# A chunked state-space scan feeding a two-layer MLP: the exponents of the first ten chunks from rows of cumulated logs

## The chip, the cores and the metric

One core of one Trainium2 chip. The metric is the device time of one execution in microseconds (us). Three runs of the kernel before stand beside the profiled one. Engines go by the profile's names: PE (TensorE; PEld is its weight load), DVE (VectorE), ACT (ScalarE), POOL (GpSimd), SP (the queue that issues nearly all DMAs).

## The reference

Four batches, eight heads, 768 positions, head size 32, state size 16. The scan gives rows of 256 values for 3072 tokens, which an MLP of 2048 hidden values takes in.

```python
log_a = np.log(np.clip(a, 1e-06, 1.0))
for c in range(nc):                        # chunks along the sequence
    cum = np.cumsum(la, axis=-1)           # la: the chunk's logs
    L = np.exp(cum[:, :, :, None] - cum[:, :, None, :]) * causal
    M = np.einsum('bhin,bhjn->bhij', Cc, Bc) * L
    y = M @ xc + (Cc @ state) * np.exp(cum)
    state = exp(sum(la)) * state + (Bc * exp(cum[-1] - cum)).T @ xc
h = x @ w_in                               # x: the scan's rows, 3072 x 256
out = (h - np.tanh(h)) @ w_out             # 256 -> 2048 -> 256
```

## The kernel before

**The scan.** It uses 28 chunks of its own: seven along the sequence for each of the four batches (six of 112 tokens, one of 96), chunk number `ck` counting batches fastest. A chunk's tile has 128 columns of keys: 16 for the carried state, which enters as 16 further tokens, and 112 for its own. For each of the eight heads a 128 x 112 matrix `lt` = exp(cumulated log of the query - that of the key), cut to the causal half, is multiplied by C B^T, and PE multiplies it by the x rows into `y` (L637). The chunks lie in groups of two, which share a load of B and C (`bc`, L265), of x (L277) and of B in rows (`braw`, L286).

Three ways of making `lt` stand side by side:

- *Chunks 0 to 3* (`first_tile`, L435 to L492). POOL lays out each head's logs as a masked 128 x 128 matrix `lm` (L443), four heads at a time; PE writes a mask of -32768 (`eye` times `never`, L448) and adds `lm` times `upto`, a triangle of ones (L451). That gives the differences of the sums, masked, in a PSUM bank (`cp`). ACT takes the exponential (L467), four heads in one instruction; PE makes C B^T in the bank group `att` (L461), and DVE multiplies (L471), again four heads at a time.
- *Chunks 4 to 9* (`chunk_a`, L494). The sums of all chunks are made once as rows (`pr`, L1032), copied, cut by DVE into three bf16 parts (L1042 to L1048), sent to memory (L1051) and fetched back by eight DMAs into `lt_c` and `rt_c` (L1056, L1058), tiles that ACT and DVE have filled with 1 and with 0 or -1 (L991, L995). Four bf16 matmuls of 9 rows each (L507), two heads to a matmul, give the exponents in one half of each of four banks of `att`, and four of 32 rows (L512) C B^T in the other half. ACT takes the exponential of all eight heads (L516), DVE multiplies (L520), POOL zeroes what is not causal (`cut`, L532).
- *Chunks 10 and later* (`chunk_l`, L535) load the rows of sums broadcast from memory, and ACT adds the key's sum as a bias (L550).

**The MLP.** Tiles of tokens, four of 256 and four of 512 columns. `mm1` (L756, L763) multiplies by the first weights into a bank `ph`; ACT takes tanh (L794), DVE subtracts (L798); `mm2` (L834, L844) multiplies by the second weights into `o`. The weights arrive as 64-bit numbers, two halves of each load (`raw`, L296); `conv` (L314) puts them together on ACT (L325) and DVE (L330 to L352). Most products go in three passes of a rounded part and a rest (`wh`, `wl`, `xh`, `xl`). The first tile, with the first two pairs of weight blocks, runs in plain float32 (L756, L834); its x is `xf` (L601). The first four tiles are swept over the weights together, as these come in.

**What sets the order.** Nothing is issued where it is written. Each step is recorded with its engine, an assumed cost and what it reads and writes (`Order.__call__`, L89); `search` (L198) schedules the records 16 times with random disturbance from a seed, keeps the shortest schedule, and issues the steps in that order. `urge` moves a step forward. Each engine then runs its list in order, and waits where data or a buffer is missing. Buffers come in rings: `ph` two banks, `po0` and `po1` one each, `att` one group of four banks, `lt` four, `raw` two, `bc` and `x` three.

## Time and profile before

| | us |
|---|---|
| median of three runs | 324.19 (323.92 to 324.30) |
| the profiled execution's own time | 324.25 |
| its span, first to last instruction | 322.6 |
| outside the span | 1.65 |
| busy in the span: PE, PEld | 313.7, 255.3 |
| busy in the span: DVE, ACT, POOL | 215.3, 210.3, 60.6 |

Busy time counts instructions at work, overlaps once. The timeline gives start, duration, engine, line, what is written and read, and in brackets how long the engine had idled before and what ended that. Where a row has a count, its duration is that of the whole stretch. A float32 matmul is two instructions in the profile (two passes), and one in the program's order; a bf16 or fp32r one is one in both.

### The profile page before, as it was taken

The numbers are of one execution on the slowest core, as the hardware profiler recorded it, in microseconds if no ns is written. First come the engines' busy times: TensorE is split into PE (matmuls) and PEld (weight loads), VectorE is DVE, ScalarE is ACT, GpSimd is POOL, SyncE is SP. The second block draws the span as 40 slices with busy tenths as digits, with TensorE's granted clock in tenths as the row PEclk, the third lists the DMA queues.
The fourth block names the chain that finished last, engine by engine and source line by source line (L and its number), as shares of the span: only waits on it lengthen the run. The fifth ranks groups of instructions, "written<-read, shape, count | busy, mean of one in ns | idle before, by whom it ended". The sixth has DMA issues, their size and how long they took to land.

```text
span 322.6 us, 5757 instructions
## 1 busy us (share of the span) xinstructions
PE 313.7 (97%) x2160; PEld 255.3 (79%) x2160; DVE 215.3 (67%) x314; ACT 210.3 (65%) x471; POOL 60.6 (19%) x94
## 2 busy tenths in 40 slices
...
GB/s 205 195 238 325 173 162 307 183 94 346 89 65 66 30 98 272 48 241 5 205 0 207 16 0 209 1 2 226 168 61 0 2 0 0 68 1 0 2 0 65
DMA packets 15451, 35.27 MB, mean 109 GB/s; under 512 B 2464, under 2 KB 4416, under 8 KB 15424
## 3 DMA queue, kind: packets, MB, share of 16 engines
...
q8 instruction: 17, 0.28, 0.4%
q14 instruction: 10, 0.08, 0.1%
...
## 4 chain that ended last, share of the span: by engine, by line
PE 91%; DVE 5%; ACT 2%; issue 1%
PE ph L763 39%; PE o L844 38%; PE o L834 3%; PE y L704 3%; PE att L678 3%; PE y L637 1%; PE warm L1003 1%; DVE lt L471 1%; ACT lt L550 1%; DVE lt L520 1%; DVE wv L345 1%; PE att L461 1%; PE cp L451 1%; ACT lt L516 1%; DVE wm L338 1%
## 5 line engine op out<-in xcount | busy, mean ns | idle before, releaser
L798 DVE TENSOR_TENSOR g<-ph,g 128x512 f32<-128x512 f32 x96 | 65.7, 688 | 52.1 <-ACT g L794 52.0
L794 ACT ACTIVATE g<-ph 128x512 f32<-128x512 f32 x96 | 57.3, 598 | 48.7 <-PE ph L763 47.8
L808 DVE TENSOR_TENSOR gl<-g,gh 128x512 fp32r<-128x512 f32 x88 | 62.7, 715 | 31.0 <-ACT gh L802 29.5
L763 PE MATMUL ph<-xh,wh 128*128 128x512 f32 (+1 forms) x200 | 76.0, 382 | 0.0
L763 PE MATMUL ph<-xh,wl 128*128 128x512 f32 (+1 forms) x200 | 74.8, 377 | 0.0
L802 ACT CAST gh<-g 128x512 fp32r<-128x512 f32 x88 | 54.4, 620 | 28.3 <-DVE g L798 26.4
L844 PE MATMUL o<-gh,wh 128*128 128x512 f32 x176 | 69.2, 393 | 0.0
L844 PE MATMUL o<-gl,wh 128*128 128x512 f32 x176 | 68.5, 389 | 0.0
L844 PE MATMUL o<-gh,wl 128*128 128x512 f32 x176 | 68.5, 389 | 0.0
L763 PE MATMUL ph<-xl,wh 128*128 128x512 f32 (+1 forms) x200 | 59.0, 376 | 0.0
L532 POOL TENSOR_SCALAR_AFFINE_SELECT lt<-lt 128x896 f32<-128x896 f32 (+1 forms) x24 | 23.3, 969 | 128.4 <-ACT lt L550 118.3
L763 PEld LDWEIGHTS ph<-xh,wh 128*128 128x128 f32 x200 | 37.6, 188 | 7.6 <-issue 0.6
L763 PEld LDWEIGHTS ph<-xh,wl 128*128 128x128 f32 x200 | 37.6, 188 | 6.8
L763 PEld LDWEIGHTS ph<-xl,wh 128*128 128x128 f32 x200 | 36.7, 188 | 7.0
L550 ACT ACTIVATE lt<-lt,ncum 128x112 f32<-128x112 f32 (+1 forms) x144 | 41.7, 375 | 0.0
L844 PEld LDWEIGHTS o<-gh,wh 128*128 128x128 f32 x176 | 33.0, 188 | 7.8 <-issue 0.8
L844 PEld LDWEIGHTS o<-gl,wh 128*128 128x128 f32 x176 | 33.0, 188 | 6.9
L844 PEld LDWEIGHTS o<-gh,wl 128*128 128x128 f32 x176 | 33.1, 188 | 6.7
L684 DVE TENSOR_TENSOR lt<-att,lt 128x896 f32<-128x896 f32 (+1 forms) x18 | 18.9, 1052 | 0.0
L888 POOL DMA_DIRECT2D pt<-part x12 | 11.1, 1023 | 41.1 <-ACT part L885 38.1
L834 PE MATMUL o<-g,wf 128*128 128x256 f32 x64 | 15.4, 384 | 1.4 <-ACT x L578 0.9
L605 ACT CAST xh<-y 128x224 fp32r<-128x224 f32 (+4 forms) x18 | 7.3, 413 | 13.1 <-DVE s L711 10.6
...
## 6 DMA issues: line engine op xcount, KB each, us to landing
...
```

Of the source, the lines that this page charges most:

```text
L532: nc.gpsimd.affine_select(out=k["l"][:, :, 0:q], in_=k["l"][:, :, 0:q], pattern=[[0, H], [1, q]], compare_op=ALU.is_ge, fill=0.0, base=N, ...
L550: nc.scalar.activation(k["l"][:, h, 0:q], k["l"][:, h, 0:q], AF.Exp, bias=ncum[:, h, ck : ck + 1])
L678: nc.tensor.matmul(out=a_[:, i], lhsT=bb[r], rhs=cc[r, :, 0 : qlen(ck)], start=True, stop=True)
L684: nc.vector.tensor_tensor(out=l, in0=chs[j]["a"], in1=l, op=ALU.mult)
L763: nc.tensor.matmul(out=ph[:, i * w : i * w + w], lhsT=w_[:, u, 0, k, j * P : (j + 1) * P], rhs=(xh, xl)[p][:, k, ts], start=p == 0 and k = ...
L794: nc.scalar.activation(g[:, 0:used], gs[t, f][0][:, 0:used], AF.Tanh)
L798: nc.vector.tensor_tensor(out=g, in0=ph, in1=g, op=ALU.subtract)
L802: nc.scalar.copy(gh[:, 0:used], gs[t, f][1][:, 0:used])
L808: nc.vector.tensor_tensor(out=gl[:, 0:used], in0=g[:, 0:used], in1=gh[:, 0:used].bitcast(F32), op=ALU.subtract)
L834: nc.tensor.matmul(out=po[t, seg][e], lhsT=wf[:, u, 256 * j + e * P : 256 * j + (e + 1) * P], rhs=gs[t, f][1][:, i * w : i * w + w], start ...
L844: nc.tensor.matmul(out=po[t, seg][e], lhsT=w_[:, u, 1, j, e * P : (e + 1) * P], rhs=g[:, i * w : i * w + w], start=f == seg[0] and k == 0 ...
L888: op("POOL", 1.0, lambda e=e: nc.gpsimd.dma_start(out=pts[m][:, e], in_=obs[t, e], accum_op=ALU.add), r=[name, n_pt[2 * m], n_pt[2 * m + 1 ...
```

## The change

All ten of the first chunks now go one way; `first_tile`, `lm`, `eye`, `never`, the bf16 parts, their memory copy `cum3` and the ten DMAs that wrote and fetched it are gone.

- `twins`: ACT takes the logs of the first ten chunks a second time into `twin`, each value four times (320 columns).
- `rows_of(g)`, for chunks 0 to 3, 4 to 7 and 8 to 9: four small float32 matmuls per chunk, 32 columns of `twin` times `upto`, put the cumulated logs of each pair of heads at the partitions where the exponents' matmuls read them. For g = 0, ACT writes `lt_c` and DVE `rt_c` (two instructions) straight from that bank, in float32. For g = 1 and 2, ACT first copies a rounded part (`high`), DVE adds the rest for alternate rows (`fn_y`), and ACT and DVE make `lt_c` and `rt_c` in fp32r from the result. Columns of signs and ones (`sel`) choose per partition what becomes a sum and what 1, 0 or -1; DVE makes them with nine small instructions (`sels`).
- `chunk_a` now holds for chunks 0 to 9. `att` is one group of banks for all ten, with two halves that are tracked apart: exponents (`room(0)`) and C B^T (`room(1)`). The exponents of chunk ck + 1 are issued right behind C B^T of chunk ck. Their four matmuls have 8 rows, in float32 for chunks 0 to 3 and fp32r after that. Exponential, product and cut then handle eight heads in one instruction each, for the first four chunks too.
- The column sums `pq`, which were in the bank of `pr`, have a slot of `po0`. The rows that are sent to memory for the later chunks stay, in a buffer of the ring `pt` in place of `ob`.
- The seed of the search is another. Lines after L57 have new numbers.

```diff
-FIRST = 4
-    ROUNDS, JITTER, SEED, EARLY, LOOK = 16, 0.3, 266, 8.0, 0.5
+    ROUNDS, JITTER, SEED, EARLY, LOOK = 16, 0.3, 9, 8.0, 0.5
-    def first_tile():
...
+    def rows_of(g):
+        cks = range(4 * g, min(4 * g + 4, JOINT))
...
+            for c, ck in enumerate(cks):
+                for i in range(4):
+                    nc.tensor.matmul(out=pk[32 * i : 32 * i + 32, c], rhs=upto, start=True, stop=True,
+                                     lhsT=twin[:, 4 * H * ck + 8 * i : 4 * H * ck + 8 * i + 32])
...
+            nc.scalar.copy(misc["t", g].bitcast(F32R), misc["pk", g][:, 0 : len(cks)])
...
+            nc.vector.scalar_tensor_tensor(out=t, in0=t, scalar=sel[:, 9:10], in1=misc["pk", g][:, 0 : len(cks)],
+                                           op0=ALU.mult, op1=ALU.add)
...
+            nc.scalar.activation(lt_c[g], source(), AF.Identity, bias=sel[:, 1:2], scale=sel[:, 0:1] if g else sel[:, 6:7])
...
+            nc.vector.tensor_scalar(out=rt_c[g][:, w], in0=source()[:, :, N:P], scalar1=sel[:, (2 if g else 7) + w : (3 if g else 8) + w],
+                                    scalar2=sel[:, 4 + w : 5 + w], op0=ALU.mult, op1=ALU.add)
...
+    def exps(ck, early):
+        k, g, ex = chs[ck], ck // 4, room(0)
...
+            for i in range(4):
+                r = slice(32 * i, 32 * i + 8)
+                nc.tensor.matmul(out=ex[:, i], lhsT=lt_c[g][r, ck - 4 * g], rhs=rt_c[g][r, :, ck - 4 * g], start=True, stop=True)
...
+            nc.scalar.activation(k["l"].rearrange("p (i w) q -> p i w q", i=4), ex, AF.Exp)
...
 chunk_a
-        op("PE", 0.65, fn_p, r=[d["n_bc"], "lt_c", "rt_c"], w=[n_a])
-        op("ACT", 0.92, fn_e, r=[n_a], w=n_l)
-        op("DVE", 1.08, fn_m, r=[n_a], w=n_l)
-        op("POOL", 1.4, lambda: cut(ck), w=n_l)
+        if ck == 0:
+            fn, r, then = exps(0, True)
+            op("PE", 0.55, fn, r=r, w=[n_e], urge=urge)
+            then()
+        fn_e, r_e, then = exps(ck + 1, early) if ck + 1 < JOINT else (None, [], lambda: None)
+        if early:
+            op("PE", 0.6, fn_p, r=[d["n_bc"]], w=[n_b], urge=urge)
+            op("PE", 0.55, fn_e, r=r_e, w=[n_e], urge=urge)
+        elif fn_e:
+            op("PE", 0.7, lambda: (fn_p(), fn_e()), r=[*r_e, d["n_bc"]], w=[n_e, n_b])
...
+        then()
+        op("DVE", 1.08, fn_m, r=[n_b], w=k["n_l"], urge=urge)
+        op("POOL", 1.1, lambda: cut(ck), w=k["n_l"], urge=urge)
...
 start of the program
+    op("ACT", 0.46, twins, r=["al", "a", "tab"], w=["twin"])
     op("ACT", 0.4, lambda: nc.scalar.activation(la.rearrange("p h (c b) -> p c b h", b=NB), a_sb, AF.Ln), r=["a", "tab"], w=["la"])
+    op("DVE", 0.9, sels, r=["idn"], w=["sel"])
-    op("ACT", 0.9, ones, w=["lt_c"])
-    for w in range(2):
-        op("DVE", 0.85, lambda w=w: signs(w), r=["par"], w=["rt_c"])
...
+    rows_of(0)
...
-    op("DVE", 1.4, lambda: [split(i) for i in range(1, 6) if i != 4], r=["rows"], w=["parts"])
-    for i in range(2):
-        op("SP", 0.42, lambda i=i: put_parts(i), r=["parts"], w=["cum3"], dma=KB)
+    rows_of(1)
+    rows_of(2)
...
-    first_tile()
+    for ck in chunks[0]:
+        chunk_a(ck, True)
+        chunk_y(ck)
```

Here is where the issued order differs, at two places and on one queue. PE before, from the warm-up matmuls on, through the differences of chunks 0 and 1 (`cp`, the bank that ACT reads; the number behind it is the half of the heads):

```order
L1003 MATMUL warm<-const-float32-1.0 32x128 x8
L1032 MATMUL pr<-upto,la 112x128 x2
L1037 MATMUL pr<-la,upto 128x224
L448 LDWEIGHTS eye
L448 MATMUL cp_0_181<-never,eye 128x4x112
L451 MATMUL cp_0_181<-upto,lm_0_170 128x112 x4
L1037 MATMUL pq_194<-la,after 128x224
L448 LDWEIGHTS eye
L448 MATMUL cp_1_200<-never,eye 128x4x112
L451 MATMUL cp_1_200<-upto,lm_1_176 128x112 x4
L448 LDWEIGHTS eye
```

The same place on PE now (L450 is `rows_of`, L491 the exponents, L512 C B^T, L644 `y` of chunk 0):

```order
L1006 MATMUL warm<-const-float32-1.0 32x128 x8
L450 MATMUL rows_174<-upto,twin 32x128 x16
L1032 MATMUL pr<-upto,la 112x128 x2
L450 MATMUL rows_205<-upto,twin 32x128 x16
L491 MATMUL att_117<-rt_c_113,lt_c_110 128x224 x4
L512 MATMUL att_117<-bc_140 128x224 x4
L450 MATMUL rows_242<-upto,twin 32x128 x8
L491 MATMUL att_117<-rt_c_113,lt_c_110 128x224 x4
L512 MATMUL att_117<-bc_140 128x224 x4
L1037 MATMUL pq<-la,upto 128x224
L491 MATMUL att_117<-rt_c_113,lt_c_110 128x224 x4
L644 MATMUL y_280<-lt_240,x_143 32x112 x8
```

The eight masks and 32 full matmuls of `cp` are gone; 40 matmuls of 32 columns and the exponents' own stand there, and the first `y` follows before the third chunk's C B^T.

DVE before, from the sums to the products of chunk 1 (L471; `wm` and `wv` are weight conversion):

```order
L1042 COPY both<-pr 112x256
L1046 CAST parts<-both 112x2x128
L1048 TENSOR_TENSOR both<-both,parts 112x256
L1046 CAST parts<-both 112x2x128
L1044 TENSOR_TENSOR parts<-both,parts 112x2x128
L1066 TENSOR_SCALAR ncum<-pr 128x224
L330 TENSOR_SCALAR wm_210<-raw_147 128x512
L335 TENSOR_SCALAR wv_206<-wv_206 128x512
L338 SCALAR_TENSOR_TENSOR wm_210<-wv_206,wm_210 128x512
L345 SCALAR_TENSOR_TENSOR wv_206<-wv_206,wm_210 128x512
L471 TENSOR_TENSOR lt_196<-att_239,lt_196 128x4x112 x2
L352 TENSOR_TENSOR wl<-wv_206,wh 128x512
```

DVE there now, up to the product of chunk 2 (L516 is the product, L328 to L343 weight conversion, L459 `fn_y`, L469 `rt_c`):

```order
L328 TENSOR_SCALAR wm_194<-raw_138 128x512
L469 TENSOR_SCALAR rt_c_113<-rows_174,sel 128x448 x2
L1045 COPY rows<-pr 112x256
L333 TENSOR_SCALAR wv_222<-wv_222 128x512
L336 SCALAR_TENSOR_TENSOR wm_194<-wv_222,wm_194 128x512
L343 SCALAR_TENSOR_TENSOR wv_222<-wv_222,wm_194 128x512
L516 TENSOR_TENSOR lt_240<-att_117,lt_240 128x8x112
L459 SCALAR_TENSOR_TENSOR high_252<-high_252,sel,rows_242 128x256
L459 SCALAR_TENSOR_TENSOR high_232<-high_232,sel,rows_205 128x512
L516 TENSOR_TENSOR lt_262<-att_117,lt_262 128x8x112
L1052 TENSOR_SCALAR ncum<-pq 128x224
L469 TENSOR_SCALAR rt_c_114<-high_232,sel 128x448 x2
```

A conversion of the first weights (L328, which waits for `raw`) now stands ahead of `rt_c` on DVE, and the two `fn_y` and the next `rt_c` among the products.

On SP, `raw` (L296, now L294), which stood behind the two `bc` of the first groups, is the first load behind `a`, and its second half is the fifth; before, that half stood behind the two writes of the bf16 parts (L1051).

More of the change, by code (lines that the diff above doesn't have):

```diff
@@ L458, in fn_p, with chunk_a @@
+    def chunk_a(ck, early=False):
+        d, k, pr_ = grp[ck // CPG], chs[ck], room(1)
+        n_e, n_b = misc["att"]
+        urge = URGE if early else 0.0
+        def fn_p():
             bb, cc = operands(ck)
@@ L658, in chunk_y @@
         else:
-            op("PE", cost, fn, r=r, w=w)
+            op("PE", cost, fn, r=r, w=w, urge=URGE if ck < len(chunks[0]) else 0.0)
         moved = []
@@ L922, in tile_ssm_moe @@
     laf = la.rearrange("p h c -> p (h c)")
-    pidf = cp.tile([P, 2], F32, name="pidf")
-    par = cp.tile([P, 2], F32, name="par")
+    twin = p2.tile([P, 4 * H * JOINT + 32], F32, tag="wv", name="twin")
+    pidf = cp.tile([P, 4], F32, name="pidf")
+    sel = cp.tile([P, 10], F32, name="sel")
     ncf = cp.tile([P, N], F32, name="ncf")
-    eye = cp.tile([P, P], BF16, name="eye")
-    never = cp.tile([P, P], BF16, name="never")[:, 0:Q]
     idn = cp.tile([P, N], F32, name="idn")
@@ L932, in tile_ssm_moe @@
     wdec = cp.tile([P, H, NCK], F32, name="wdec")
-    both = p2.tile([P, 2, 2, P], F32, tag="ob", name="both")
-    rows, rest = both[:, 0], both[:, 1]
-    parts = p2.tile([P, 2, 3, P], BF16, tag="ob", name="parts")
-    lt_c = cp.tile([P, NEAR.stop - NEAR.start, P], BF16, name="lt_c")
-    rt_c = cp.tile([P, 2, NEAR.stop - NEAR.start, P], BF16, name="rt_c")
+    rows = p1.tile([P, 2, P], F32, tag="pt", name="rows", bufs=NM)
+    lt_c = [cp.tile([P, min(4, JOINT - 4 * g), P], F32R if g else F32, name=f"lt_c{g}") for g in range(3)]
+    rt_c = [p2.tile([P, 2, 4, Q], F32R if g else F32, tag="ob", name=f"rt_c{g}") for g in range(2)]
+    rt_c.append(cp.tile([P, 2, JOINT - 8, Q], F32R, name="rt_c2"))
     cumr = dr.tile([NCK, H, P], F32, name="cumr")
-    cum3 = dr.tile([3, H, NCK, P], BF16, name="cum3")
     def ones_a():
@@ L987, in stay @@
                                   in_=idn[0:N].unsqueeze(1).broadcast_to([N, CPG * H, N]))
-    def ones():
-        v = lt_c.rearrange("p c m -> p (c m)")
-        nc.scalar.copy(v, nc.const_aps.tensor(1.0, (P, 1), F32).broadcast_to(v.shape))
-    def signs(w):
-        v = rt_c[:, w].rearrange("p c q -> p (c q)")
-        nc.vector.tensor_scalar(out=v, in0=nc.const_aps.tensor(1.0, (P, 1), F32).broadcast_to(v.shape),
-                                scalar1=par[:, w : w + 1], scalar2=None, op0=ALU.mult)
     def warm():
```

177 lines of the change are left out of this document (66 added, 111 removed).

## The prediction

> **What bounds the kernel now.** I read the page first, then the chain of waits, then a table of two stretches, then the timeline of the first 60 us.
>
> ```profile
> PE 313.7 (97%) x2160; PEld 255.3 (79%) x2160; DVE 215.3 (67%) x314; ACT 210.3 (65%) x471; POOL 60.6 (19%) x94
> PE 91%; DVE 5%; ACT 2%; issue 1%
> 0.00:60.00 60.00, 54.94 (x696) 44.56 (x696) 50.71 (x80) 43.76 (x102) 24.91 (x47) 1.00 0.66 216
> 60.00:318.75 258.75, 258.74 (x1468) 210.74 (x1464) 163.88 (x234) 166.53 (x369) 35.66 (x47) 1.00 0.28 84
> 318.75:322.60 3.85, 0.00 (x0) 0.00 (x0) 0.69 (x1) 0.00 (x0) 0.00 (x0) 1.00 0.36 136
> ```
>
> After the stretch and its length, the table gives the busy time of PE, PEld, DVE, ACT and POOL. From 60 us until the last matmul PE idles 0.01 us; the end, 3.85 us, is a copy and a store. So the span is PE's work, plus 60 - 54.94 = 5.06 us in which PE waits ahead of 60 us, plus the end. Only two things can change it: PE's work, and those 5.06 us. DVE comes next in the first stretch, 50.71 of 60 us.
>
> **PE's work.** The masks and differences of chunks 0 to 3 (L448, L451), C B^T and exponents of chunk 4 (L507, L512), and two `y` (L637):
>
> ```profile
> 15.39 0.36 PE L448 MATMUL cp<-never,eye 128*128 128x448 bf16 x1
> 15.59 1.04 PE L451 MATMUL cp<-upto,lm 128*128 128x112 f32 x8
> 16.46 0.35 PE L448 MATMUL cp<-never,eye 128*128 128x448 bf16 x1
> 18.21 0.97 PE L637 MATMUL y<-lt,x 128*32 128x112 f32 x32
> 20.56 0.28 PE L507 MATMUL att<-rt_c,lt_c 9*128 9x224 bf16 x4
> 20.67 0.57 PE L512 MATMUL att<-bc 32*128 32x224 f32 x8
> 21.16 1.99 PE L756 MATMUL ph<-xf,wv 128*128 128x256 f32 x8
> ```
>
> *Removed:* one group of four heads takes 16.46 - 15.39 = 1.07 us from start to start; eight groups are 8.56 us.
>
> *Added, rows:* `rows_of` has 40 float32 matmuls of 32 columns, like `y`, where four column strips run side by side: 16 in 0.97 us for 112 moving columns, 0.97 x 128/112 = 1.11 for 128, so 2.5 x 1.11 = 2.77 us.
>
> *Added, exponents of chunks 0 to 3:* four float32 matmuls over 224 columns in separate row strips, the form of C B^T. That takes 21.16 - 20.67 = 0.49 us start to start, 0.57 alone; since most stand alone here, 0.55 x 4 = 2.2 us. C B^T itself is there before and after.
>
> *Changed, exponents of chunks 4 to 9:* fp32r for bf16, 8 rows for 9. No row shows fp32r in row strips. The MLP's fp32r passes take one instruction, like bf16, and one of 256 columns lasts 0.28 us here, about what four bf16 strips of 224 take together:
>
> ```profile
> 34.04 0.28 PE L763 MATMUL ph<-xh,wh 128*128 128x256 f32 x1
> ```
>
> I take 0. The bounds: at best a little under the 20.67 - 20.56 = 0.11 us now, a gain of 0.1 in all; at worst the float32 price, 0.49 - 0.11 = 0.38 more for each of six chunks, 2.3 us.
>
> Sum: 2.77 + 2.2 - 8.56 = -3.6 us of PE work.
>
> **DVE's and ACT's work**, which must keep up:
>
> ```profile
> 1.86 0.15 DVE L975 TENSOR_SCALAR par<-pidf 128x1 f32<-128x1 f32 x1
> L1046 DVE CAST parts<-both 112x256 bf16<-112x256 f32 x2 | 1.0, 483 | 0.1
> 3.32 1.85 DVE L995 TENSOR_SCALAR rt_c<-const-float32-1.0,par 128x768 bf16<-128x768 f32 x2
> 7.01 1.03 DVE L1048 TENSOR_TENSOR both<-both,parts 112x256 f32<-112x256 f32 x1
> 8.41 0.42 DVE L1044 TENSOR_TENSOR parts<-both,parts 112x256 bf16<-112x256 f32 x1
> 11.65 1.16 DVE L471 TENSOR_TENSOR lt<-att,lt 128x448 f32<-128x448 f32 x2
> 16.66 0.42 DVE L335 TENSOR_SCALAR wv<-wv 128x512 f32<-128x512 f32 x1
> 22.26 1.09 DVE L520 TENSOR_TENSOR lt<-att,lt 128x896 f32<-128x896 f32 x1 [0.79 <-ACT lt L516]
> ```
>
> DVE loses the signs (1.85), the splitting (1.0 + 1.03 + 0.42 = 2.45) and eight half products (4 x 1.16 = 4.64): 8.9 us. (The row of L1046 is from the groups by line: its two instructions take 1.0 us.) It gains four whole products (4.36), two `rt_c` from PSUM at 0.58, as half a row of L471 (1.16), `fn_y` over 512 and 256 elements at L471's rate (0.65 + 0.35), three lots of `rt_c` from SBUF at L335's rate (0.82 for chunks 4 to 7, 0.5 for 8 and 9), and nine instructions on one column at 0.15, 1.35, which lie ahead of a wait for a load (below): 9.2 us. Nothing is won there. ACT loses the ones and eight half exponentials, and gains four whole ones, the second logs, two rounded copies and three `lt_c`:
>
> ```profile
> 2.21 0.81 ACT L991 CAST lt_c<-const-float32-1.0 128x768 bf16<-128x768 f32 x1
> 3.44 0.61 ACT L1010 ACTIVATE la<-a_sb 128x224 f32<-128x224 f32 x1 [0.41 <-DVE a_sb L968]
> 8.36 0.68 ACT L325 ACTIVATE wv<-raw 128x512 f32<-128x512 f32 x1 [0.90 <-DMA raw<-w_d]
> 15.32 0.53 ACT L467 ACTIVATE lt<-cp 128x448 f32<-128x448 f32 x1
> 21.31 0.92 ACT L516 ACTIVATE lt<-att 128x896 f32<-128x896 f32 x1 [0.26 <-PE att L512]
> ```
>
> That is 0.81 + 8 x 0.53 = 5.05 against 4 x 0.92 + 0.7 (L1010 with more columns) + 3 x 0.6 + 2 x 0.38 = 6.9 us: 1.9 more, 45.7 of 60, covered. POOL loses eight `lm` and the masks and gains four cuts of 0.98; it idled most of the time. If a cut finds POOL at `bw` it comes some 0.5 late, which I allow for below.
>
> **The start, step by step.** The new order puts a weight conversion, which waits for `raw`, ahead of `rt_c` on DVE, and behind it everything that DVE does for chunk 0. When does `raw` land?
>
> ```profile
> 1.72 0.91 SPq L265 DMA_DIRECT2D bc<-bc_d  x2
> 2.67 0.43 SPq L296 DMA_DIRECT2D raw<-w_d  x1
> 9.77 0.50 SPq L296 DMA_DIRECT2D raw<-w_d  x1
> 14.74 0.69 ACT L325 ACTIVATE wv<-raw 128x512 f32<-128x512 f32 x1 [1.41 <-DMA raw<-w_d]
> ```
>
> Both waits for it end with the landing: 14.74 - 9.77 = 4.97 us with little ahead, 8.36 - 2.67 = 5.69 behind two `bc`. It is issued at 1.72 now, so it lands at 6.7 (7.4 at the worst; 5.5 if the first place in the queue saves more). PE has `rows` of chunks 0 to 3 by 6 (warm-up ends at 4.4). Then, with the durations above and 0.2 to 0.3 us per change of engine: conversion to 7.15, both `rt_c` to 8.3, exponents on PE to 9.1, exponential to 10.3. DVE meanwhile copies the sums and converts (0.42, and L335, L338 and L345 in the old numbers, 0.42 and two of 0.7, for which a row stands below) to about 10.55, and makes the first product by 11.65. It then has two `fn_y` (1.0), the product of chunk 1 (1.09), `ncum` (0.4, the size of L1044), two `rt_c` (0.82) and the product of chunk 2 (1.09): 16.0. With 0.5 for POOL at `bw`, the cut runs to 17.6, `y` to 18.4, its copy to 19.0, and the first tile's matmuls start at about 19.25, against 21.16 (L756): 1.9 us earlier. This is DVE's chain now, not PE's.
>
> ```profile
> 21.16:61.11 39.95, 36.77 (x528) 29.72 (x524) 35.04 (x45) 31.93 (x80) 12.13 (x16) 1.00 0.67 225
> 24.77 0.98 POOL L532 TENSOR_SCALAR_AFFINE_SELECT lt<-lt 128x896 f32<-128x896 f32 x1
> 25.80 0.59 PE L637 MATMUL y<-lt,x 128*32 128x112 f32 x16 [0.48 <-POOL lt L532]
> 29.90 1.99 PE L834 MATMUL o<-g,wf 128*128 128x256 f32 x8 [0.86 <-ACT x L578]
> 32.45 0.28 PE L507 MATMUL att<-rt_c,lt_c 9*128 9x224 bf16 x4 [0.56 <-DVE lt L520]
> 61.11 0.50 PE L763 MATMUL ph<-xh,wh 128*128 128x512 f32 x1
> ```
>
> **From there to the packed part.** At that point PE will have left over, compared with before, C B^T of chunk 4 and `y` of chunk 3 (0.5 + 0.45), and will have done one `z` early (0.35): 0.6 us more to do. Between 21.16 and 61.11 PE waits 39.95 - 36.77 = 3.2 us now, at the rows just shown and their like. Some of these go: the exponents of the next chunk no longer wait for the product of the last (0.56), and the copies into x wait for a load (0.86) that is issued earlier when the first `y` are. SP loses ten issues of the parts, with the waits on them, but now holds x of groups 3 and 4 until `y` of chunks 1 and 3 are through, and the second half of the third weights behind the latter; by my walk that half is issued at about 25.4 and lands at 30.4, one us after ACT could take it, which shifts a conversion and not PE. I let half of the 3.2 go. 1.9 - 0.6 + 1.6 = 2.9 us. The other way of counting gives the same: 3.6 us less work, and PE waits in the first 60 us not 5.06 but about 5.6, since in the first 20 us it now waits for DVE between the small steps; 3.0 us. I take 3.0.
>
> The span becomes 322.6 - 3.0 = 319.6, the execution 321.25 with the 1.65 outside; the median before was 324.19, 0.06 under the profiled run, so 321.2.
>
> **The rivals.**
>
> 1. *DVE takes PE's place as the bound (0.16).* For: DVE's work stays at 50 us while PE's shrinks, and only DVE's lead at the start can be kept. The same conversion lasts 0.69 or 1.00 us:
>
> ```profile
> 9.98 1.00 DVE L338 SCALAR_TENSOR_TENSOR wm<-wv,wm 128x512 uint32<-128x512 uint32 x1
> 17.11 0.69 DVE L338 SCALAR_TENSOR_TENSOR wm<-wv,wm 128x512 uint32<-128x512 uint32 x1
> ```
>
> If three or four of DVE's new steps stretch like that, 1.0 of the 1.9 goes, and the waits stay: 1.9 - 1.0 = 0.9 us, 323.3. The Trainium skill (SBUF — State Buffer, Who interferes with whom) holds that a DVE instruction with two SBUF inputs, or one in a two-port mode, and a GpSimd instruction block each other; L338 has two SBUF inputs and POOL was at work beside the slower one, so the trace agrees so far. Against: POOL has less to do than before.
>
> 2. *fp32r strips cost as float32 (0.06).* 2.3 us of the 3.0 go: 323.5.
>
> 3. *PE's clock falls in the thinned start (0.06), slower.* For: the first matmuls run slowly,
>
> ```profile
> 0.85 3.59 PE L1003 MATMUL warm<-const-float32-1.0 128*32 128x128 f32 x16 [0.85 <-PEq L1187]
> ```
>
> 0.224 us per pass of 128 columns, against 1.04/8 = 0.13 for 112 at 15.59, so PE has a slow state at half the rate. Between 7.3 and 19.25 PE will have some 8.5 us of work: 5 exponents and 4 C B^T at 0.55, `rows` of the last two chunks 0.55, two column sums 1.1, three `y` 1.5, `z` 0.4. At half rate that is 8.5 more, of which the 3.5 us of waiting hide at most that much; with 1.7 until it is fast again, the front comes 6.7 later: 321.2 + 6.7 = 327.9. It decides from about half of that on, 3 us. The Trainium skill (TensorE: Matmul & The Clock Gate, Part 1) says that the clock halves after an idle window of about 3.4 us, and also that frequent small idling can make it oscillate; by the first rule nothing happens here. Against: my longest single wait is 1.4 us, and between 25 and 30 us PE was busy 3.66 of 5 us, about the 8.5 of 12 expected here, with L756 in it at its usual pace.
>
> ```profile
> 25.00:30.00 5.00, 3.66 (x85) 2.65 (x81) 4.97 (x7) 3.60 (x9) 2.59 (x4) 1.00 0.98 332
> ```
>
> 4. *The new seed's order opens gaps behind 60 us (0.10).* PE waits 0.01 us there now, so it can only lose: a few waits like those above, 0.5 to 0.9 each, take 1 to 2.5 us of the gain, 322.2 to 323.7.
>
> **How the numbers follow.** The forecast, 321.2, has 0.62. Its own bounds: `raw` at 5.5 (1.2 better), all waits of 3.2 gone (1.6 better), not both in full with DVE so near, so 1.8 better, 319.4; `raw` at 7.4 and two more waits, 1.5 worse, 322.7. Rivals 1, 2 and 4 lie between 322.2 and 323.7. The range 319.4 to 323.7 leaves out rival 3 and the tails. This kernel's measurement tells 0.2% (0.65 us) from no change, so "same" is 323.5 to 324.8: half of rival 2, a part of 1 and 4, 0.08. Slower: rival 3 and a remainder of 4, 0.08. Faster: 0.84.
>
> **What would show it.** In the new profile: PE's busy time about 310; the exponents of chunks 4 to 9 at 0.1 to 0.15 us apart from the C B^T beside them (0.5 would be rival 2); the first weight conversion on DVE near 6.7 and the first tile's matmuls near 19.3; the first 512-column matmul near 58 and not 61.1; PE still without waits behind it. A pass of 128 columns in `rows` or `y` at 0.22 between 8 and 20 us would be rival 3, DVE busy without a break from 10 to 57 us with PE waiting rival 1. The prediction is wrong if PE's work falls by 3.6 us and its waits grow by as much.

## The result, and the profile after

The changed kernel takes 333.44 us (333.29 to 333.55, four runs) where the kernel before takes 324.06 (323.48 to 324.30): ratio 1.0292, 95% interval 1.0274 to 1.0310. The forecast was 321.2. A ratio below is the time against the kernel before, with its 95% interval in brackets; the mean granted clock of a run stands beside its time where it matters; one run each of `fill` and `rows_late`, with a mean clock of 0.65 and 0.56, is left out.

The page of the changed kernel: busy time, granted clock in 40 slices of 8.3 us, chain.

```profile
PE 318.1 (96%) x2200; PEld 255.7 (77%) x2200; DVE 219.1 (66%) x321; ACT 211.1 (64%) x472; POOL 62.9 (19%) x87
PEclk9657899999999999999999999999999999999999
PE 90%; DVE 6%; ACT 1%; DMA 1%; issue 1%; DVEq 0%; ACTq 0%; SPq 0%
```

The table of stretches of the changed kernel, the last four cut where the clock changes (granted clock third from the end):

```profile
0.00:60.00 60.00, 50.59 (x674) 37.35 (x675) 46.71 (x78) 37.11 (x83) 23.56 (x38) 0.83 0.60 195
60.00:327.60 267.60, 267.55 (x1527) 218.37 (x1526) 171.76 (x244) 174.02 (x390) 39.29 (x49) 1.00 0.29 85
7.93:11.34 3.41, 1.61 (x32) 1.07 (x32) 3.32 (x6) 2.50 (x5) 0.47 (x1) 1.00 1.06 345
11.34:28.41 17.07, 14.26 (x141) 8.31 (x142) 10.77 (x15) 8.73 (x18) 5.91 (x8) 0.50 0.46 148
35.23:38.65 3.42, 1.37 (x23) 1.03 (x16) 2.69 (x5) 2.14 (x4) 1.37 (x1) 1.00 0.92 285
38.65:42.06 3.41, 3.41 (x10) 2.70 (x9) 3.41 (x6) 1.97 (x6) 1.51 (x2) 0.50 1.00 362
```

All of the loss lies ahead of 60 us; behind it PE waits 0.05. In front PE waits 60 - 50.59 = 9.41 us (5.06 before), and its busy time, which should have fallen to 310.1, rose to 318.1: for 17.1 and 3.4 us it ran at half clock. Against the forecast: 8.0 us more busy, 3.8 more waiting, 11.8 of the 12.2 us; of the rest, 0.3 lie outside the span (333.45 - 331.5 = 1.95 us, 1.65 before).

The timeline of the changed kernel, chunks 0 to 2. L491 are the exponents, L512 C B^T (a set below is the four matmuls of either), L495 the exponential, L516 the product; they all touch `att`:

```profile
6.02 0.43 DVE L328 TENSOR_SCALAR wm<-raw 128x512 uint32<-128x512 uint32 x1 [1.23 <-DMA raw<-w_d]
7.14 0.78 ACT L466 ACTIVATE lt_c<-rows,sel 128x512 f32<-128x512 f32 x1 [1.14 <-DVE rt_c L469]
7.95 0.74 DVE L469 TENSOR_SCALAR rt_c<-rows,sel 128x448 f32<-128x448 f32 x1 [0.85 <-ACT lt_c L466]
8.75 0.66 PE L491 MATMUL att<-rt_c,lt_c 8*128 8x224 f32 x8 [1.70 <-DVE rt_c L469]
9.23 0.56 PE L512 MATMUL att<-bc 32*128 32x224 f32 x8
9.86 0.92 ACT L495 ACTIVATE lt<-att 128x896 f32<-128x896 f32 x1 [0.91 <-PE att L512]
10.81 1.09 DVE L516 TENSOR_TENSOR lt<-att,lt 128x896 f32<-128x896 f32 x1
11.95 1.13 PE L491 MATMUL att<-rt_c,lt_c 8*128 8x224 f32 x8 [1.59 <-DVE lt L516]
13.15 0.92 ACT L495 ACTIVATE lt<-att 128x896 f32<-128x896 f32 x1 [1.55 <-PE att L491]
14.12 1.13 PE L512 MATMUL att<-bc 32*128 32x224 f32 x8 [1.04 <-ACT lt L495]
15.39 1.09 DVE L516 TENSOR_TENSOR lt<-att,lt 128x896 f32<-128x896 f32 x1 [2.44 <-PE att L512]
16.54 1.13 PE L491 MATMUL att<-rt_c,lt_c 8*128 8x224 f32 x8 [0.24 <-DVE lt L516]
18.50 1.13 PE L512 MATMUL att<-bc 32*128 32x224 f32 x8
19.70 0.92 ACT L495 ACTIVATE lt<-att 128x896 f32<-128x896 f32 x1 [4.42 <-PE att L512]
21.93 1.09 DVE L516 TENSOR_TENSOR lt<-att,lt 128x896 f32<-128x896 f32 x1 [3.73 <-PE att L491]
26.41 2.97 PE L763 MATMUL ph<-xf,wv 128*128 128x256 f32 x8
29.98 0.44 PE L491 MATMUL att<-rt_c,lt_c 8*128 8x224 f32 x4
```

Two things are to be read. First, turns: PE, ACT and DVE use `att` one after the other, though exponents and C B^T are different halves. Exponents of chunk 1 (11.95) wait for the product of chunk 0, which reads the other half; C B^T (14.12) waits for the exponential; the exponential of chunk 2 (19.70), whose exponents were there at 17.67, waits for C B^T at 18.50. Second, from 11.34 on, where the clock halves, the same sets take 1.13 in place of 0.66.

### The profile page after: what moved, and what is told of

Read it like the earlier page. It is cut to its first block, busy times and chain, and to the rows that moved or that the text cites. A ratio compares the mean times of both kernels' runs of the same rounds, so it can differ in the third digit from the quotient of the medians.

```text
span 331.5 us, 5837 instructions
## 1 busy us (share of the span) xinstructions
PE 318.1 (96%) x2200; PEld 255.7 (77%) x2200; DVE 219.1 (66%) x321; ACT 211.1 (64%) x472; POOL 62.9 (19%) x87
## 3 DMA queue, kind: packets, MB, share of 16 engines
q0 software_dynamic: 1728, 3.15, 5.6%
## 4 chain that ended last, share of the span: by engine, by line
PE 90%; DVE 6%; ACT 1%; DMA 1%; issue 1%; DVEq 0%; ACTq 0%; SPq 0%
PE ph L770 39%; PE o L851 37%; PE o L841 5%; PE y L711 3%; PE att L685 3%; DVE lt L516 2%; DMA raw<-w_d 1%; PE att L512 1%; PE att L491 1%; PE y L644 1%; DVE wm L336 1%; ACT lt L495 1%; DVE rt_c L469 1%; DVE wv L333 0%; DVE wf L343 0%
## 5 line engine op out<-in xcount | busy, mean ns | idle before, releaser
L539 POOL TENSOR_SCALAR_AFFINE_SELECT lt<-lt 128x896 f32<-128x896 f32 (+1 forms) x28 | 30.4, 1086 | 144.2 <-ACT lt L557 119.5
L841 PE MATMUL o<-g,wf 128*128 128x256 f32 x64 | 17.0, 419 | 0.2 <-DVE xl L615 0.2
L516 DVE TENSOR_TENSOR lt<-att,lt 128x896 f32<-128x896 f32 x10 | 10.9, 1088 | 8.8 <-PE att L491 4.9
```

The costliest lines, as they stand in the source:

```text
L516: nc.vector.tensor_tensor(out=lt, in0=pr_, in1=lt, op=ALU.mult)
L539: nc.gpsimd.affine_select(out=k["l"][:, :, 0:q], in_=k["l"][:, :, 0:q], pattern=[[0, H], [1, q]], compare_op=ALU.is_ge, fill=0.0, base=N, ...
L841: nc.tensor.matmul(out=po[t, seg][e], lhsT=wf[:, u, 256 * j + e * P : 256 * j + (e + 1) * P], rhs=gs[t, f][1][:, i * w : i * w + w], start ...
```

## Experiments: turns or clock

Edits are against the changed kernel unless said otherwise. "PE waits" are those ahead of 60 us in the profile.

### own_chunk

```diff
-        op("PE", 0.55, fn_e, r=r_e, w=[n_e], urge=urge)   # exponents of chunk ck + 1, behind C B^T of ck
+        fn_e, r_e, then = exps(ck, early)                 # exponents of ck, ahead of C B^T of ck
+        op("PE", 0.7 if ck > 3 else 1.1, lambda: (fn_e(), fn_p()), r=[*r_e, d["n_bc"]], w=[n_e, n_b], urge=urge)
```

> The exponents of a chunk are issued with C B^T of the same chunk, as one step; rows of logs and everything else as changed (the schedule is searched anew with the same seed). Shared-bank theory: four changes of hands per chunk become three, a chunk takes some 3.5 us in place of 4.4, PE is still thin and its clock still halves for a while: 326 to 331 us. Clock-alone theory: about 333, since PE is no denser. Order theory: anything from 322 to 335, as the order is a new one.

332.16 us (331.98 to 333.34), ratio 1.0235 [1.0203, 1.0268], clock 0.972, PE waits 8.24. The theory of shared banks expected 331 at most and is missed by 1.2 us. Products start at 11.40, 16.49, 21.01 and 25.04, against 10.81, 15.39, 21.93 and 27.53: still 4 to 5 us apart. Issuing with the neighbour costs 1.3 us against this, in which the other order has a part, and is not the cause.

### seed_266

Only the seed: `SEED = 266` for 9.

> The changed kernel with the old seed of the search. Shared-bank and clock theories: 330 to 336 us, with products some 4.4 us apart and a half clock. Order theory: within 1 us of 324.

332.70 us (331.94 to 333.01), 1.0250 [1.0221, 1.0280], clock 0.967. Between these two seeds the order accounts for 0.7 us.

### banks_apart and tiles_apart

Both put exponents into two banks and C B^T into two others, so that no bank is shared; all four matmuls of a set then use row strips 0 and 1 (heads 4 to 7 get other heads' values) and go two by two. `banks_apart` keeps one tile, `tiles_apart` has two:

```diff
-        return misc["room"][:, :, 0 : 4 * Q]...[:, :, 2 * i : 2 * i + 2]
+        return misc["room"][:, 2 * i : 2 * i + 2, 0 : 4 * Q]...          # banks_apart
+        return misc["room"][i][:, :, 0 : 4 * Q]...                       # tiles_apart: [tile(2 banks), tile(2 banks)]
```

> Exponents go to banks 0 and 1 of the group, C B^T to banks 2 and 3; for that all four matmuls of a set use row strips 0 and 1, twice each, so that heads 4 to 7 get the values of other heads (left out: their own). Order and sizes of all instructions unchanged. PE pays for it: two pairs one after the other in place of four strips at once, some 0.5 us more for each of 14 float32 sets and 0.1 for six fp32r sets, 7.6 us. Shared-bank theory: the waits of PE's exponents for the product of the chunk before and of ACT for C B^T go, the first products lie 2 to 2.7 us apart, the clock does not halve before 30 us or only briefly, and the time is 323 to 329 us in spite of the 7.6. Clock-alone and order theories: spacing as before, 4.4 us or more, and 333 to 341 us.

> Like banks_apart, with the same extra PE work and the same order on every engine, but exponents and C B^T are two tiles of two banks each, so that PE's exponents of the next chunk wait for ACT alone and no longer for DVE's product, and ACT's exponential no longer for C B^T. Theory of turns (a tile in PSUM passes from engine to engine, and both halves are one tile): the first products come 2 to 3 us apart in place of 4.6 to 8.7 in banks_apart, the granted clock stays at 1.00 or halves for under 7 us, and the time is 9 to 14 us under banks_apart, 326 to 331 us; PE's waits in the first 60 us fall from 8.0 to about 5. Clock-alone theory: spacing shrinks little, the time stays within 3 us of banks_apart (337 to 341). DVE theory (DVE's own work spaces the products): likewise within 3 us.

`banks_apart`: 339.89 us (338.99 to 342.82), 1.0491 [1.0434, 1.0548], clock 0.955 to 0.962. `tiles_apart`: 332.35 (328.12 to 332.41; the profiled run, at clock 0.969, took 334.21 and is not among them), 1.0213 [1.0142, 1.0284]. The theory of shared banks had expected 323 to 329 of `banks_apart`, and is wrong there. Stretch and timeline of `banks_apart`:

```profile
0.00:60.00 60.00, 52.01 (x576) 39.71 (x580) 41.09 (x71) 33.48 (x70) 19.94 (x35) 0.80 0.51 166
12.90 1.86 PE L491 MATMUL att<-rt_c,lt_c 8*128 8x224 f32 x8 [1.57 <-DVE lt L516]
15.78 1.86 PE L512 MATMUL att<-bc 32*128 32x224 f32 x8 [1.01 <-ACT lt L495]
```

The same of `tiles_apart` (L492 and L513 are the two sets), with the stretches around its fall of the clock:

```profile
0.00:60.00 60.00, 56.51 (x645) 44.31 (x649) 45.62 (x77) 37.00 (x79) 23.43 (x38) 0.83 0.59 190
8.97:12.38 3.41, 3.15 (x40) 2.49 (x40) 3.34 (x7) 2.09 (x4) 0.21 (x1) 1.00 1.05 333
12.38:32.86 20.48, 19.92 (x176) 13.65 (x176) 13.74 (x18) 10.45 (x23) 8.62 (x10) 0.50 0.42 139
9.23 1.02 PE L492 MATMUL att<-rt_c,lt_c 8*128 8x224 f32 x8 [1.67 <-DVE rt_c L470]
10.09 0.92 PE L513 MATMUL att<-bc 32*128 32x224 f32 x8
10.94 0.64 PE L451 MATMUL rows<-upto,twin 128*32 128x128 f32 x16
11.51 1.05 PE L492 MATMUL att<-rt_c,lt_c 8*128 8x224 f32 x8
12.40 1.86 PE L513 MATMUL att<-bc 32*128 32x224 f32 x8
```

The waits stay with separate banks and go with separate tiles: PE waits 7.99 and 3.49 us. In the two profiled runs PE is busy for the same 325 us, and the spans, 337.1 and 332.5 us, lie as far apart as the waits, 4.5 us; the medians lie 7.5 us apart, the runs of `tiles_apart` that make it having a higher clock (0.974). So the order is kept for the PSUM tile as a whole, by the program, and not for the bank. The Trainium skill (PSUM — Partial Sum Buffer, PSUM bank collisions raise a hardware error) asks for an order only where two engines touch the same bank and quadrant; by that `banks_apart` had no need to wait, and the trace shows that it does.

But the clock fell all the same in three of the four runs, with PE busy 3.15 of the 3.41 us before, and for 20.48 us where under 7 were expected. And of one kernel, the run at clock 0.995 took 328.12, those at 0.974 332.35 and 332.41: 4.2 us for 0.021 x 331 = 7 us of clock lost.

### fill and fill_light

Idle places filled by full 128 x 128 float32 matmuls into a bank that nobody reads: 36 (5 behind the last rows, 4 behind the exponents and 3 behind C B^T of chunks 1 to 3) and 12 (3, 2, 1).

```diff
+            nc.tensor.matmul(out=misc["fill"][:, i % 4], lhsT=upto, rhs=upto, start=True, stop=True)
```

> Extra full 128x128 float32 matmuls on PE into a bank that nobody reads (36 in all), behind the rows of chunks 8 and 9 and behind the exponents and C B^T of chunks 1 to 3; the order of everything else is that of the changed kernel. Shared-bank theory (exponents and C B^T lie in the same four banks, whose users take turns, so that a chunk takes some 4.4 us; PE is thinned by that and its clock halves as a second step): the granted clock stays at 1.00 until 30 us, the products of chunks 0 to 3 still lie 3.5 to 4.4 us apart, and the time falls by most of half of the 14.9 us in which PE was busy at half clock from 11.7 to 28.6 us, to 326 to 329 us. Clock-alone theory (the waits would have been harmless at full clock): 324 or less. Order theory (the new seed's order is at fault): 333, as the order is the same.

> Fewer full matmuls as filling: 3 behind the rows of chunks 8 and 9, 2 behind the exponents and 1 behind C B^T of chunks 1 to 3, 12 in all at about 0.22 us, in a profile at the usual clock. Theory of turns: if these keep the clock at 1.00 to 30 us, the products of chunks 0 to 3 still lie about 4 us apart and the time is 327 to 330 us, the part of the loss that the half clock makes; if the clock falls all the same, 331 to 335. Clock-alone theory: with the clock kept, 322 to 325.

`fill`: 332.31 us (330.73 to 334.03), 1.0243 [1.0188, 1.0299]. `fill_light`: 332.18 (331.33 at clock 0.995, 332.18 and 332.26 at 0.989; a fourth run, in which the fillers did not hold the clock, took 336.87 at 0.964), 1.0243 [1.0218, 1.0268]. The theories expected 326 to 329 and 327 to 330 with the clock held, the clock alone 325 or less: each too low. The 333 that the theory of the order gave for `fill` is nearest, but `seed_266` speaks against it. Stretches of `fill_light`:

```profile
0.00:60.00 60.00, 51.78 (x703) 39.24 (x704) 47.68 (x79) 38.27 (x87) 23.48 (x39) 0.94 0.62 202
9.40:12.82 3.42, 2.70 (x40) 1.75 (x36) 3.39 (x5) 1.91 (x4) 0.88 (x2) 1.00 1.06 323
12.82:16.23 3.41, 2.53 (x25) 1.44 (x23) 1.91 (x4) 1.96 (x3) 0.76 (x2) 1.00 0.99 348
26.47:29.89 3.42, 1.35 (x15) 1.09 (x16) 3.35 (x5) 1.06 (x5) 2.14 (x2) 1.00 0.39 137
29.89:33.30 3.41, 3.41 (x23) 2.08 (x21) 2.88 (x4) 2.15 (x3) 1.72 (x2) 0.50 0.02 5
```

The clock holds to 29.89 us; yet the products of chunks 0 to 3 start at 10.78, 14.42, 19.82 and 25.31, not much closer than in the changed kernel (10.81, 15.39, 21.93, 27.53). They are 3.6 to 5.5 us apart at full clock, of which the three fillers between two of them are 0.7, and the rows say that DVE idles for PE's turn:

```profile
14.42 1.09 DVE L529 TENSOR_TENSOR lt<-att,lt 128x896 f32<-128x896 f32 x1 [1.50 <-PE att L523]
19.82 1.09 DVE L529 TENSOR_TENSOR lt<-att,lt 128x896 f32<-128x896 f32 x1 [2.58 <-PE att L500]
```

In the second row the product of chunk 2 waits for the exponents of chunk 3 (L500), which lie in the other half.

### rows_late and seed_9_before

`rows_late` is the kernel before for chunks 0 to 3 and the rows for chunks 4 to 9, own chunk, old seed. `seed_9_before` is the kernel before with the new seed.

```diff
+    first_tile()                                   # rows_late: chunks 0 to 3 as before
+        op("PE", 0.65, fn_p, r=[d["n_bc"], f"lt_c{ck // 4}", ...], w=[n_a])   # chunks 4 to 9: lt_c, rt_c from rows_of
-    ROUNDS, JITTER, SEED, EARLY, LOOK = 16, 0.3, 266, 8.0, 0.5
+    ROUNDS, JITTER, SEED, EARLY, LOOK = 16, 0.3, 9, 8.0, 0.5     # seed_9_before, alone
```

> One part of the change alone: chunks 0 to 3 as in the kernel before (differences by PE, their own banks), chunks 4 to 9 with rows of logs made by PE, rounded part and rest, and fp32r exponents, but exponents and C B^T of the same chunk issued together, as before; no copy of parts to memory. Schedule searched anew with the old seed. Theory of turns: no thinned PE at the start, clock at 1.00, 24 small matmuls more on PE (1.7 us) and as much work on DVE: 323 to 327 us. Theory that the rows themselves, or fp32r exponents, cost the time: 329 us or more.

> The kernel before with the new seed of the search: all theories but one 323 to 327 us, within 1% of the kernel before; order theory: 330 or more.

`rows_late`: 327.53 us (326.57 to 327.53), 1.0098 [1.0072, 1.0123], clock 0.995 to 0.998. `seed_9_before`: 328.97 (326.89 to 329.87), 1.0131 [1.0091, 1.0170], clock 0.990 to 0.999. Both lie above the 323 to 327 expected, by 0.5 and 2.0 us, and short of the rivals' 329 and 330. Of the 9.4 us lost, 5.9 come with chunks 0 to 3, by difference; the other 3.5 are no more than an order alone can cost, 4.9 in `seed_9_before`. An order alone can open a thin place too, and its price goes with the clock: 326.89 at 0.999, 329.87 at 0.990.

### halves, halves_fill and halves_266

If long turns are the trouble, shorter ones help: one tile for row strips 0 and 1, one for 2 and 3, exponentials and products in halves; then with the fillers of `fill_light`, then with the old seed.

```diff
-            misc["room"] = ps_a.tile([P, 4, 4 * P], F32, tag="att", name="att0")
+            misc["room"] = [ps_ab.tile([P, 2, 4 * P], F32, tag=f"att{j}", name=f"att{j}") for j in range(2)]
+        for j in range(2):
+            op("DVE", 0.6, lambda j=j: fn_m(j), r=[n_b[j]], w=[k["n_l"][j]], urge=urge)
```

> The changed kernel with two PSUM tiles of two banks in place of the one of four: row strips 0 and 1 (heads 0 to 3) in one, strips 2 and 3 in the other, four matmuls side by side as before; exponentials and products of chunks 0 to 9 in two halves each. Theory (turns on one tile): a turn in one half is a set on PE 0.55, half an exponential 0.53, a set 0.55, half a product 0.58 and four changes of engine of 0.2: 3.0 us against the 4.4 now, and the other half runs beside it. Products of chunks 0 to 3 come about 3 us apart, the last of the ten near 42 us (54.5 now), PE waits about 6 in the first 60 us, and the time is 326 (322 to 329). Rival (the clock alone): PE is still thin in the start, its clock halves at about 12 us as now, 331 to 333. Rival (what DVE and ACT have to do bounds the start): half instructions cost more in sum, nothing is won, 333 or above.

> The kernel with halves, with the 12 full matmuls of fill_light as filler (3 behind the last rows, 2 behind the exponents and 1 behind C B^T of chunks 1 to 3, in a bank of their own, nobody reads them; 12 x 0.21 = 2.6 us of added PE work, the larger part in waits). Theory (turns first, clock second): the clock stays at 1.00 for the first 30 us at least, and the time is within 2 us of halves, below it if halves still showed half clock: 325 (321 to 328). Rival (the clock alone): 4 us or more under halves. If both causes of the loss are named rightly, this one is within 3 us of the forecast of 321.2 plus what filler lies on PE's path (up to 2.6).

> The kernel with halves with the old seed of the planner. The order's part: seed 9 and 266 were 0.7 us apart in the changed kernel, 4.5 us in the kernel before. Theory (turns): within 3 us of halves, both clearly under 333. Rival (the order is what decides): over 3 us apart.

335.09 us (1.0343 [1.0325, 1.0361]), 337.67 (1.0400 [1.0359, 1.0442]) and 331.54 (1.0235 [1.0212, 1.0259]): the forecasts of 326 and 325 missed by 9 and 12 us. The edit did not shorten the turns, as rows of `halves` show:

```profile
12.06 0.62 DVE L521 TENSOR_TENSOR lt<-att,lt 128x448 f32<-128x448 f32 x1 [0.88 <-PE att L492]
16.07 0.62 DVE L521 TENSOR_TENSOR lt<-att,lt 128x448 f32<-128x448 f32 x1 [1.35 <-PE att L492]
```

PE still writes a set into both tiles in one step. The second half of chunk 0's product (12.06) had to wait for chunk 1's exponents (L492), and so on: second halves come 4.0 us apart (12.06, 16.07, 20.14), where 3.0 were expected. DVE idles ahead of them, so the rival that expected 333 or above, with DVE and ACT as the bound, has the number of `halves` and not its reason. The three kernels say little for or against turns. With the old seed the halves are 1.2 us better than whole turns (`seed_266`), with the new one 1.7 worse, and the two are 3.6 us apart, as the rival of the order had it (over 3): the order does more than the splitting. The table of stretches of `halves_fill`:

```profile
0.00:60.00 60.00, 53.84 (x641) 39.84 (x642) 47.84 (x86) 35.71 (x83) 22.89 (x36) 0.83 0.56 179
11.03:14.44 3.41, 2.77 (x24) 1.66 (x23) 2.53 (x5) 2.20 (x5) 1.19 (x1) 1.00 1.04 341
14.44:28.09 13.65, 13.21 (x132) 8.51 (x132) 9.24 (x16) 6.14 (x14) 5.53 (x7) 0.50 0.34 106
```

PE was busier here (2.77 us) than `fill_light` in either of its first two stretches (2.70, 2.53), and lost the clock where that kernel kept it. Busy time does not decide.

### What the clock goes by: fill_8rows, fill_again, halves_fill36

The stretches at half clock last 3.41, 6.83, 13.65, 17.07, 20.48, 23.89 or 30.72 us, multiples of 3.41. The Trainium skill (TensorE: Matmul & The Clock Gate, Part 1) describes windows of that length that run on by themselves, and a clock that halves after an idle one. The length agrees; that the window must be idle does not: it was busy for 33 to 93% where the clock fell.

I gave each matmul the share of the array that it fills: active rows/128 x active columns/128 x its time at full clock for its moving columns (0.107 us for 128 columns of a float32 instruction; the fillers of `fill_again` show (1.38 - 0.94)/4 = 0.11; as much for 256 columns of an fp32r pass, which in `rows_late` start 0.12 us apart). Sums over the stretches of 3.41 us ahead of 300 us in 17 profiles, from the rows of all matmuls:

| stretch of 3.41 us, clock still full | stretches | share of the array | PE busy |
|---|---|---|---|
| clock halves at its end | 24 | 0.19 to 0.37 | 0.33 to 0.93 |
| clock stays | 1380 | 0.36 and up | 0.55 and up |

The two groups meet at 0.36 to 0.37; a share is good to a few hundredths, since it depends on where in its record a matmul's time is put. Rows alone (falls up to 1.1, strips side by side counted in full, stays from 0.4) or columns alone (1.4 and 0.4) do not part them. At half clock it came back after 0.35 or more and stayed low up to 0.36. In the kernel before, the five stretches from 5.16 to 22.23 us have 0.65 to 0.89; in the changed kernel the one from 7.93 to 11.34 has 0.26. `tiles_apart` had 0.29 ahead of its fall: 16 instructions of `rows` at 0.107/4, 16 of exponents at 0.187 x 8/128 and 8 of C B^T at 0.187 x 32/128 make 0.99 us of 3.41. To test it, the fillers of `fill_light` with 8 rows of the array in place of 128; beside it `fill` once more, for its profile, and `halves` with the same 36 fillers:

```diff
-            nc.tensor.matmul(out=misc["fill"][:, i % 4], lhsT=upto, rhs=upto, start=True, stop=True)
+            nc.tensor.matmul(out=misc["fill"][:, i % 4], lhsT=upto[0:8], rhs=upto[0:8], start=True, stop=True)
```

> The kernel fill_light with each of its 12 filler matmuls on 8 of the 128 rows of the array: the same number of moving columns, so about the same time on PE, a sixteenth of the array's work. Theory (the clock goes by the array's work in stretches of 3.41 us): the clock halves in the first 15 us as in the changed kernel, mean granted clock 0.96 to 0.98, time 333 to 335.5 (333.4 and some of the 2.6 us of fillers). Rival (the clock goes by how long PE is busy): as fill_light, full clock for the first 28 us, mean 0.985 to 0.995, 331.3 to 332.5.

> The kernel fill (36 full matmuls as filler), for its profile. Theory (clock and turns both count): mean clock 0.989 to 1.0, 330.7 to 334 as before; with the clock at 1.00 through the first 28 us the products of chunks 0 to 3 still come 3.5 us or more apart, and PE, beside its 7.6 us of fillers, waits 4 to 7 us in the first 60. Rival (the clock alone): products 2 to 2.5 us apart as forecast, once the clock is held.

> The kernel halves with the 36 full fillers of fill: turns half as long, and the clock held. Theory (turns still count when the clock is held): 1.5 to 4 us below fill_again, 327 to 330, with products about 3 us apart. Rival (turns do not matter once the clock is held; DVE's and ACT's work or PE's fillers bound the start): within 1 us of fill_again or above it, since ACT and DVE do the same work in twice as many instructions.

`fill_8rows`: 334.41 us (333.54 to 334.97), 1.0319 [1.0299, 1.0339], clock 0.969 to 0.973. Stretches, and the fillers' row:

```profile
8.12:11.53 3.41, 2.48 (x38) 1.81 (x38) 3.34 (x6) 2.50 (x5) 0.71 (x1) 1.00 1.05 320
11.53:32.01 20.48, 19.24 (x162) 14.28 (x162) 11.95 (x17) 8.80 (x18) 7.22 (x10) 0.50 0.46 152
10.35 0.93 PE L445 MATMUL fill<-upto 8*128 8x128 f32 x6
```

The same fillers of `fill_light` on the full array, and of `fill_again`:

```profile
10.27 0.94 PE L445 MATMUL fill<-upto 128*128 128x128 f32 x6
```

```profile
10.17 1.38 PE L445 MATMUL fill<-upto 128*128 128x128 f32 x10
14.12 0.94 PE L445 MATMUL fill<-upto 128*128 128x128 f32 x6
0.00:60.00 60.00, 53.98 (x728) 42.07 (x729) 47.05 (x78) 37.60 (x84) 21.94 (x37) 0.94 0.59 192
```

Same place, same 0.93 us: with 8 rows the clock halves at 11.53 for 20.5 us, at an array share of 0.27 and PE busy 73%; with 128 rows it holds, at 0.45 and 0.40 in the first two stretches of `fill_light`, PE busy 79% and 74%. On 128 rows the same instructions of the stretch of `fill_8rows` would make 0.45. All four runs of `fill_8rows` have the clock and the time that the array's work forecast (0.96 to 0.98, 333 to 335.5). Array work decides, not busy time.

`fill_again`: 332.20 us (330.50 to 333.41), 1.0248 [1.0220, 1.0276]. Its six runs order by clock: 330.50 and 330.71 at 1.000, 332.05 and 332.36 at 0.995, 333.19 and 333.41 at 0.99. With the clock held to 30.33 us its products still start at 10.68, 14.32, 20.30, 26.11. The rival of the clock alone, 2 to 2.5 us apart, falls; seven fillers between two products, 1.5 us, are part of these distances. `halves_fill36`: 336.59 (334.55 to 338.80), 1.0383 [1.0343, 1.0423], 334.55 to 335.62 at 0.987 to 0.989, 1 to 2.5 us above `fill_again` at 0.989 and 0.990. Forecast were 327 to 330, and the rival that expected no gain has it right: the halves do not pay even there. PE waits less (6.16 us in `halves_fill`, 9.41 in the changed kernel) and is busy longer at half clock; what else makes them slow was not taken further.

### tiles_fill: both causes away

`tiles_apart` (heads 4 to 7 as there) with 19 full fillers (4, 3, 2).

> The kernel tiles_apart (two tiles, so no turns; four matmuls two by two, so about 6 us more PE work) with 19 full fillers on all 128 rows in chunks 0 to 3 and behind the last rows (19 x 0.21 = 4.0 us more). Theory (turns and clock together are the miss): mean clock 0.985 or more, PE waits 4.5 us or less in the first 60, and the time is 329 to 332, which less the 10.1 us of work that the experiment adds is 319 to 322, the forecast's 321.2 within 2 us. Rival (something else, as DVE's work or the order, holds the start back): the fillers do not find room and PE still waits 6 us or more at full clock, 334 or above.

Seven runs in two groups: 330.06 to 330.17 at clock 0.998 to 1.000 (four), ratio 1.0197 [1.0180, 1.0214], and 343.76 to 344.16 at 0.955 (three, the profile among them). The first group is in line with the forecast: 330.1 - 10.1 us of added work = 320.0. Of these 10.1, about 6 are an estimate from the rows above (0.86 us from set to set in `tiles_apart` where the changed kernel has 0.48, in 14 float32 sets, and 0.1 in six others). The subtraction takes all of it as lying on PE's path; what fills waits costs nothing, so 320.0 is the least that this says. Put as a sum, PE's work of 310.1 + 10.1, the end of 3.9 and 1.7 outside are 325.8, which leaves 4.3 us of waits where the forecast had 5.6. The run of `tiles_apart` at clock 0.995, without fillers, says the same: 328.12 - 6 = 322. The second is the same program when one stretch falls short:

```profile
8.06:11.47 3.41, 2.78 (x36) 2.31 (x37) 3.34 (x6) 2.10 (x5) 0.21 (x1) 1.00 1.04 325
11.47:42.19 30.72, 30.16 (x214) 21.76 (x215) 12.69 (x19) 10.30 (x22) 8.15 (x10) 0.50 0.31 104
```

Array share 0.35 in the first; then PE hardly idles, but strips at half clock reach 0.23 to 0.35 in eight stretches, and the clock comes back only behind the ninth, with 0.40. 13.7 us between runs of one program, 0.9 per us of clock lost. Why the runs part was not measured; that stretches run on by themselves, and so cut the start at another place each time, would fit. PE's waits at full clock could not be read, since the profile is of the other group.

### before_cut

A try to beat both: the kernel before without the mask matmuls, POOL cutting each half product instead.

```diff
-            nc.tensor.matmul(out=f[:, :, 0:Q], lhsT=eye, rhs=never.unsqueeze(1).broadcast_to([P, 4, Q]), ...
+                op("POOL", 0.55, lambda ck=ck, i=i: fn_c(ck, i), w=[k["n_l"][i]], urge=urge)
```

> The kernel before, without the mask matmuls of chunks 0 to 3: each head's differences start their own sums, and GpSimd clears what lies above the diagonal behind each half product (eight cuts of four heads), as it does for chunks 4 to 9. PE loses eight passes of 448 columns, 15.59 - 15.39 = 0.2 us each, 1.6 in all. If PE's work is what counts as in the sum of the prediction: 324.1 - 1.6 = 322.5. If the cut's 0.5 us on the way to the first y, and another order of the planner, eat that: 324 to 327 (seed 9 alone moved this kernel by 4.5).

328.09 us (327.56 to 328.41), 1.0123 [1.0104, 1.0142], clock 0.989 to 0.992, PE waits 5.87: 1.6 us of work saved, and still 4 us longer than before, above both forecasts: another order with a thin place at 26 to 29 us, behind which 6.8 us run at half clock. No kernel here beats the one before.

## Why the prediction was wrong

The price of the clock was in it; its cause was not, and a second cause was missed.

- **PE's work, -3.6 us: right.** If the 14.26 + 3.41 us busy at half clock took half, 318.1 - 8.8 = 309.3 (310.1 forecast), an estimate. An fp32r set of exponents lasts 0.44 us (at 29.98) against 0.28 in bf16, within the bound.
- **The start up to the first product: right within 0.3 us, by two misses that cancel.** `raw` at 6.02 (6.7) came 0.7 early; but ACT and DVE took turns on `rows` (1.14, then 0.85 us of waiting), and `rt_c` took 0.74 for 0.58. So the exponents were done at 9.41 (9.1) and the first product at 11.90 (11.65).
- **"the product of chunk 1 (1.09) ... and the product of chunk 2 (1.09): 16.0": this step failed.** It lets PE, ACT and DVE use the two halves of `att` side by side. The planner tracks the halves apart; what is built orders them as one tile. The product of chunk 2 ended at 23.02, the first tile's matmuls started at 26.41 (19.25). Before already showed it, in a row of its timeline that the prediction passed over: C B^T of chunk 1 waits for the products of chunk 0 (the 11.65 + 1.16 of L471), though it writes the other half.

```profile
12.85 0.31 PEld L461 LDWEIGHTS att<-bc 32*128 32x128 f32 x8 [0.28 <-DVE lt L471]
```

- **"half of PE's waits go": failed with it.** PE waits 9.41 us in place of 5.6. The prediction's own sign of being wrong, work down by 3.6 and waits up by as much, came out (up by 4.35); by itself that would have left the kernel about level with the one before. The clock made it slower.
- **Rival 3, the clock, 0.06: right in price (6.7 us) and wrong in its condition.** It got half rate from rows that show 1.5 times (0.224 against 0.13 x 128/112 = 0.15); the granted clock shows the half, 0.50. Its case against counted busy time (3.66 of 5 us before, with the clock kept). That stretch was full of work on the whole array (share 0.74 from 25.64 to 29.05); the walk put row strips there. The removed `cp` groups were 8.56 us of whole-array matmuls in the first 20 us: dropping them took the work away that held the clock. `rows_late`, which keeps them, holds it to 56 us.
- **Rivals 1 and 2 and the order: not it.** DVE is busy 46.71 of 60 us; PE waits 0.05 behind 60 us; the seed is worth 0.7; an fp32r set costs at most 0.16 more, 1 us in six.

How the 12.2 us divide: 8.0 are longer busy time, 3.8 waits. Held at full clock, the time would not fall by all of 8.0, since some would turn into waits. By `tiles_apart` (0.6 us per us of clock lost), `fill_again` (0.8) and `tiles_fill` (0.9) the 0.031 x 331.5 = 10.3 us lost here are worth 6 to 9, an estimate. The rest, 3 to 6, is put down to turns by subtraction. The run of `fill_light` at clock 0.995 speaks for the upper end: 331.33, less 1.3 for its clock and at most 2.6 for its fillers, is still 6.2 above the forecast. That turns are needed for the clock to fall is not so (`tiles_apart`). That both together make the miss rests on `tiles_fill` and the best run of `tiles_apart`, and so on the estimate of their added work.
